# Query loads in 1 KB rows with the decay applied in the cast, plain copies of the retention's output, and another order of the first loads

## The chip, the cores and the metric

The kernel runs on one core of a Trainium2 chip. The metric is device time in microseconds (us) of one execution: the median of the runs is 292.84 us (three runs, 292.4 to 293.26). The engines are TensorE (PE in the profile, PEld for its weight loads), VectorE (DVE), ScalarE (ACT), GpSimd (POOL) and SyncE (SP), which issues most of the DMAs.

## The reference, cut to what matters

```
scores = (q @ k.T) / sqrt(64)                        # 8 batches, 8 heads, 576 tokens, head size 64
gamma  = 1 - 2 ** (-5 - h)                           # one decay for each head
D      = gamma ** (i - j) for i >= j, else 0
attn   = (scores * D) @ v
x      = attn, heads side by side: 4608 tokens x 512
out    = relu(x @ w_in) ** 2 @ w_out                 # 512 -> 2048 -> 512
```

The factor gamma ** (i - j) is a product of gamma ** i, which belongs to the query's token, and gamma ** -j, which belongs to the key's. The key's part is multiplied into v while v is cast to 16 bits (line 375, line 408). The query's part can be applied to the query before the matmuls or to the output after them, since it is one factor for each token and head. A retention over long rows is carried by a state per head (the sum of k.T v so far), which is decayed by gamma ** 128 from one block of 128 tokens to the next.

## The kernel before

**Tiling.** A unit is one batch's block of 128 tokens, or the last 64 tokens of two batches together ("tail"). There are 36 units, in 18 groups of two, numbered 0 to 17. Groups 0 to 3 are "paired" (lines 391 and 456): one load brings two units in rows of 512 B, and TensorE transposes k and q. From group 4 on each unit has its own loads of k, q and v (`add_load`, line 284; 256 KB each in rows of 256 B), GpSimd casts all three (`add_unit`, line 357), and one DMA transposes k and q together into `kqT` (line 388).

**The work of one group on TensorE.** The retention is four kinds of small matmuls on quarters of the array, all issued in `quad` (line 348): scores into `psc`, masked by VectorE into `rT` (line 676); state sums into `psS`, added and decayed by VectorE (lines 695 to 703 and 449); outputs of both the state and the masked scores into `psO`, which VectorE multiplies by gamma ** i and casts into `xT` (line 732; line 565 for the paired groups). Then the feed-forward: 64 matmuls `ph` of 256 columns with w_in (line 856), for each pair of banks a Relu and a Square on ScalarE (lines 864 and 874; one Square in eight is on VectorE, line 876), and the product with w_out. Group 0 makes that product plainly: 32 matmuls of 512 columns (line 896) and two ScalarE copies of its output (line 903). Groups from `STRASSEN = 1` on use Strassen's scheme (`add_strassen`, line 912): seven products of 8 matmuls with 256 columns (line 948), 56 in all, with sums `gS` of activations on VectorE (line 925), differences `wT` of w_out made once on VectorE (line 808), and copies and additions of partial results (lines 961, 971, 1022).

**What sets the order.** `Schedule` (line 15) is a planner in Python: every task has an engine, a duration, dependencies and resources (the eight PSUM banks are the resource `ff`), and the order that comes out is written into the program, one fixed order for each engine. An instruction can wait in its engine's queue but not be overtaken. So a late operand holds up all that stands behind it on that engine.

**The first loads.** `FIRST` is the order in which the planner issues the pair loads of groups 0 to 3 (k0, q0, v0 for group 0, k2 for group 1, k4 for group 2, k6 for group 3) on SP's queue and the eight weight pieces (w0 to w3 of w_in, w4 to w7 of w_out, 1 MB of 32-bit values each, cast to 16 bits on the way) on POOL's queue. `AFTER` makes a transfer wait for another's landing, so that they share the DMA engines in the wished order:

```
FIRST = ["k0", "q0", "v0", "k2", "q2", "v2", "w0", "w1", "w2", "k4", "q4", "v4", "w3", "w4", "w5", "w6", "w7", "k6", "q6", "v6"]
AFTER = {0: ("v", 0), 3: ("k", 4), ("k", 4): 0, ("k", 6): 5}
```

That is: w0 behind v0, w3 behind k4, k4 behind w0, k6 behind w5. At the start of the program TensorE fills its waits with 34 matmuls on zeros (line 251).

Of the kernel before, what the change touches and what calls it, by code (L numbers as in the profile page):

```python
# [103 lines left out]
def kernel(  # L104
# [9 lines left out]
    nc = tc.nc  # L114
# [24 lines left out]
    STRASSEN = 1  # L139
# [38 lines left out]
    vdec = {}  # L178

    def make_vdec(kind, pos):  # L180
        t = const.tile([P, H], FP32, name=f"vdl_{kind}")
        nc.vector.tensor_scalar(out=t, in0=lnrow, scalar1=pos, scalar2=None, op0=ALU.mult)
        d = const.tile([P, H], FP32, name=f"vdec_{kind}")
        nc.scalar.activation(out=d, in_=t, func=ACTF.Exp, bias=lnscale, scale=1.0)
        vdec[kind] = d
    make_vdec("full", iota_p)
# [9 lines left out]
    heads = [(4 * n + 2 * a + b, n, a, b) for n in range(2) for a in range(2) for b in range(2)]  # L196
    lncol = const.tile([P, NP], FP32, name="lncol")
    lnrow_R = const.tile([P, NP], FP32, name="lnrow_R")
    for h, n, a, b in heads:
        nc.vector.memset(lncol[64 * b:64 * b + 64, 2 * n + a:2 * n + a + 1], lng[h])  # L200
        nc.vector.memset(lnrow_R[64 * a:64 * a + 64, 2 * n + b:2 * n + b + 1], lng[h])

    mask = const.tile([P, 64], FP32, name="mask")
    nc.gpsimd.memset(mask, 1.0)
    for c in range(2):
        nc.gpsimd.affine_select(out=mask[c * 64:(c + 1) * 64], in_=mask[c * 64:(c + 1) * 64],
                                compare_op=ALU.is_ge, fill=0.0, base=0, pattern=[[1, 64]], channel_multiplier=-1)
# [9 lines left out]
    for hp in range(NP):  # L217
        nc.scalar.activation(out=gam_f[:, hp, :], in_=iota_f, func=ACTF.Exp, scale=lncol[:, hp:hp + 1])
    gam = {"full": gam_f.rearrange("p n (c i) -> p c n i", c=2),
           "tail": gam_f[:, :, 0:64].rearrange("p n (c i) -> p c n i", c=1).to_broadcast([P, 2, NP, 64])}  # L220
# [7 lines left out]
    SPREAD = 0.1  # L228
    SQ_LATE = (1, 4, 6)
# [4 lines left out]
    FIRST = ["k0", "q0", "v0", "k2", "q2", "v2", "w0", "w1", "w2", "k4", "q4", "v4", "w3", "w4", "w5", "w6", "w7", "k6", "q6", "v6"]  # L234
    AFTER = {0: ("v", 0), 3: ("k", 4), ("k", 4): 0, ("k", 6): 5}
# [36 lines left out]
    def dma_task(key, dur, fn, deps2=(), **kw):  # L272
        t = add("SP", key, dur, fn, deps=list(last_load) + list(deps2), **kw)
        last_load[:] = [t]
        return t
# [8 lines left out]
    def add_load(u):  # L284
        kind, b, c = units[u]
        for n, (name, src) in enumerate((("k", k), ("q", q), ("v", v))):
            def fn(name=name, src=src):
                x = ld.tile([P, H, D], FP32, name=f"{name}32", tag=f"{name}32")
                tile_of[name + "32", u] = x
                if kind == "full":  # L290
# [5 lines left out]
            loaded[name, u] = dma_task(0, 1.2 if loaded else 2.1, fn, acq=("ld",) if n == 0 else ())  # L296

    def add_load_pair(name, u):
        n = "kqv".index(name)

        def fn():
# [5 lines left out]
            if (name, u) in AFTER:  # L307
                behind(t, tile_of["w", AFTER[name, u]])
            tile_of["load", name, u] = t
        kw = dict(deps2=[wcast[AFTER[name, u]][0]]) if (name, u) in AFTER else {}  # L310
        loaded[name, u] = loaded[name, u + 1] = dma_task(0, 1.81 if loaded else 2.9, fn, acq=("wst",) if name != "q" else (),
                                                         after=2.1 + LAG.get(name + str(u), 0.0), **kw)
# [3 lines left out]
    def add_weight(i):  # L316
        fb = i % 4

        def fn():
# [3 lines left out]
            if i in AFTER:  # L323
                behind(tile_of["w", i], tile_of[("load",) + AFTER[i]])
        issue = add("POOL", -90 + i, 0.9, fn, deps=issues[-1:] + ([loaded[AFTER[i]]] if i in AFTER else []),
                    lag=0.0 if i in AFTER else 1.0)
# [30 lines left out]
    def add_unit(u, base):  # L357
# [4 lines left out]
        def sorted_cast(op, out_, in_):  # L362
            op(out=out_.rearrange("p (n b a d) -> p n b a d", n=2, b=2, a=2),  # L363
               in_=in_.rearrange("p (n a b) d -> p n b a d", n=2, a=2))
# [5 lines left out]
        def fq():  # L370
            sorted_cast(nc.gpsimd.tensor_copy, tile_of["kq", u][:, 1], tile_of["q32", u])
# [7 lines left out]
        cq = add("POOL", base + 1, 0.62, fq, deps=[loaded["q", u], ck])  # L379
# [11 lines left out]
    def add_unit_pair(u, base):  # L391
# [4 lines left out]
        for i, name in enumerate("kqv"):  # L396
            xs[name] = []
            for e in range(2):
# [3 lines left out]
                def fc(name=name, e=e, eng=eng):  # L402
# [8 lines left out]
                    else:  # L411
                        engines[eng](out=t.rearrange("p (n b a d) -> p n b a d", n=2, b=2, a=2),
                                     in_=x.rearrange("p (n a b) d -> p n b a d", n=2, a=2))
# [42 lines left out]
    def add_ret_pair(g):  # L456
# [29 lines left out]
        def fk():  # L486
            ps = rT["sum"] = banks("psS")
            for hp in range(NP):
                for e in range(2):
                    for s, a in ((0, 0), (1, 1), (0, 1), (1, 0)):  # L490
                        h = 4 * (hp // 2) + 2 * a + hp % 2
# [32 lines left out]
        def inter(other):  # L524
            for n in range(2):
                for a, b in ((0, 0), (1, 1), (0, 1), (1, 0)):
                    s = a ^ other
                    if s or carry:
                        x = 2 * n + b
                        put2(s, 4 * n + 2 * a + b, before(s)[half(a), half(x)], kqT(s)[half(a), NP + x, :], a)  # L530
# [7 lines left out]
        def fo1():  # L538

            tile_of["psO", g] = banks("psO")  # L540
            for m in range(NP):
                for e in range(2):
                    for s, b in ((0, 0), (1, 1), (0, 1), (1, 0)):
                        h = 2 * m + b
                        put2(s, h, tile_of["vx", u][half(s), e, 64 * h:64 * h + 64],
                             rT[e][half(s), m % 2, 2 * (m // 2) + b, :], s)
# [47 lines left out]

    def emit_scores(g):

        tile_of["psc", g] = banks("psc")
        for s, u in enumerate(units_of(g)):
            kT = tile_of["kqT", u]
# [488 lines left out]
```

## Time and profile before

| What | Before |
|---|---|
| Median of the runs | 292.84 us |
| The profiled execution's own time | 292.84 us |
| Its span, first to last instruction | 291.1 us |
| VectorE, ScalarE, GpSimd busy | 185.2, 188.4, 85.1 us |
| DMA packets, of them under 512 B | 139437, 118144 |
| Share of 16 DMA engines taken by SP's queue | 73.7% |
| TensorE's first matmul and last matmul's end | 1.3 and 286.9 us |
| Granted TensorE clock | 0.997 |

The span is what the profile accounts for; the 1.7 us beside it lie before the first and after the last instruction. The profile gives a matmul some 0.27 us, although the next one starts after 0.11 us, because matmuls overlap in the array. So a stall of TensorE is read from the distance between two starts, not from the sum of durations.

### The profile page before, as it was taken

How to read it: one execution, taken by the hardware profiler on the slowest of the kernel's cores; microseconds unless marked ns; L12 is line 12 of the kernel's file. 1: busy time of each engine (PE TensorE's matmuls, PEld its weight loads, DVE VectorE, ACT ScalarE, POOL GpSimd, SP SyncE). 2: the span in 40 equal slices, each digit the busy share in tenths (PEclk: the TensorE clock that was granted, in tenths of full speed). 3: DMA queues.
4: the chain of work that ended last, by engine and by line, in shares of the span. 5: the costliest groups of instructions: out<-in, count | busy, mean ns of one | idle time of the engine just before them, and what ended most of it. 6: DMA issues, size and time to landing. Idle time of an engine off the chain costs nothing.

```text
span 291.1 us, 10058 instructions
## 1 busy us (share of the span) xinstructions
PE 282.5 (97%) x4346; PEld 235.7 (81%) x4346; DVE 185.2 (64%) x392; ACT 188.4 (65%) x363; POOL 85.1 (29%) x121
## 2 busy tenths in 40 slices
PE   8999899999999999999999999999999999999994
PEld 3568647788878889888888888888888888888883
DVE  3773588778475748556768757576787675455632
ACT  5459769734867575867766667585767676747830
POOL 5615306352343433252515142525141400000000
PEclk9999999999999999999999999999999999999998
DMA  7999999999899889999969698999896720202004
GB/s 200 275 226 235 177 253 250 215 220 170 220 202 231 179 178 201 190 211 221 189 150 213 112 233 182 202 222 207 193 183 181 164 75 2 74 2 74 0 6 141
DMA packets 139437, 49.94 MB, mean 172 GB/s; under 512 B 118144, under 2 KB 135040, under 8 KB 139392
## 3 DMA queue, kind: packets, MB, share of 16 engines
q1 hardware_dynamic: 134848, 44.84, 73.7%
q0 software_dynamic: 4224, 4.19, 9.2%
q8 instruction: 34, 0.56, 0.8%
q10 hardware_dynamic: 320, 0.26, 0.4%
q14 instruction: 11, 0.09, 0.1%
HBM read 36.70 MB, written 9.44 MB: 158 GB/s over the span
## 4 chain that ended last, share of the span: by engine, by line
PE 70%; DVE 1%; issue 0%; DVEq 0%
PE ph L856 34%; PE po L948 31%; PE psO L349 3%; PE psS L349 1%; PE psc L349 1%; DVE o L971 0%; DVE rT L676 0%; DVE p L1000 0%; DVEq L971 0%
## 5 line engine op out<-in xcount | busy, mean ns | idle before, releaser
L856 PE MATMUL ph<-xT,w_in 128*128 128x256 f16 x1152 | 139.7, 273 | 0.8 <-DMA w_in<-in_moe_w_in_dram 0.8
L856 PEld LDWEIGHTS <-w_in 128*128 128x128 f16 x1152 | 110.5, 98 | 15.3 <-DMA w_in<-in_moe_w_in_dram 1.4
L864 ACT ACTIVATE rl<-ph 128x512 f16<-128x512 f32 x144 | 84.6, 588 | 51.2 <-PE ph L856 49.8
L874 ACT ACTIVATE gT<-rl 128x512 f16<-128x512 f16 x118 | 74.4, 630 | 3.4
L948 PEld LDWEIGHTS <-gS 128*128 128x128 f16 x544 | 52.5, 98 | 6.4
L948 PE MATMUL po<-wT,gS 128*128 128x256 f16 x408 | 54.9, 273 | 0.0
L925 DVE TENSOR_TENSOR gS<-gT 128x512 f16<-128x512 f16 x68 | 35.5, 524 | 15.6 <-ACT gT L874 15.6
L948 PEld LDWEIGHTS <-gT 128*128 128x128 f16 x408 | 39.3, 98 | 5.6 <-issue 0.8
L925 DVE TENSOR_TENSOR gS<-gT,gS 128x512 f16<-128x512 f16 x68 | 31.0, 459 | 12.5 <-ACT gT L874 10.6
L948 PE MATMUL po<-w_out,gT 128*128 128x256 f16 x272 | 36.7, 273 | 0.6 <-DVE rT L676 0.6
L363 POOL CAST kq<-k 128x512 f16<-128x512 f32 x28 | 19.3, 690 | 51.0 <-DMA k<-in_k_dram 49.7
L375 POOL TENSOR_TENSOR v<-v,vdec_full 128x512 f16<-128x512 f32 x24 | 25.4, 1058 | 29.5 <-DMA v<-in_v_dram 27.9
L961 ACT COPY u<-po 128x256 f32<-128x256 f32 x34 | 12.5, 369 | 23.9 <-PE po L948 23.7
L363 POOL CAST kq<-q 128x512 f16<-128x512 f32 x28 | 18.1, 647 | 30.6 <-DMA q<-in_q_dram 30.1
L971 DVE TENSOR_TENSOR o<-po,u 128x256 f32<-128x256 f32 x33 | 13.9, 421 | 15.9 <-PE po L948 9.6
L732 DVE TENSOR_TENSOR xT<-psO,gam_full 128x512 f16<-128x512 f32 x28 | 18.1, 685 | 7.7 <-PE psO L349 7.6
L676 DVE TENSOR_TENSOR rT<-psc,mask 128x512 f16<-128x512 f32 x28 | 18.3, 683 | 3.2 <-PE psc L349 3.0
L971 DVE TENSOR_TENSOR o<-po,p 128x256 f32<-128x256 f32 x18 | 7.6, 423 | 18.4 <-ACT u L961 11.9
L876 DVE TENSOR_TENSOR gT<-rl 128x512 f16<-128x512 f16 x26 | 12.7, 489 | 9.3 <-ACT rl L864 9.0
L948 PE MATMUL po<-w_out,gS 128*128 128x256 f16 x136 | 18.2, 273 | 0.0
L948 PE MATMUL po<-wT,gT 128*128 128x256 f16 x136 | 17.7, 273 | 0.0
L478 DVE TENSOR_TENSOR rx<-psc,mask 128x512 f16<-128x512 f32 x16 | 10.1, 683 | 3.7 <-PE psc L349 3.7
(78 smaller groups left out, 217.2 us busy)
## 6 DMA issues: line engine op xcount, KB each, us to landing
out_dram<-o SPq DMA_DIRECT2D x32, 256.0 KB, 3.1
k<-in_k_dram SPq DMA_DIRECT2D x24, 256.0 KB, 4.2
q<-in_q_dram SPq DMA_DIRECT2D x24, 256.0 KB, 4.9
v<-in_v_dram SPq DMA_DIRECT2D x24, 256.0 KB, 4.8
pair<-in_k_dram SPq DMA_DIRECT2D x4, 512.0 KB, 5.6
pair<-in_q_dram SPq DMA_DIRECT2D x4, 512.0 KB, 8.3
pair<-in_v_dram SPq DMA_DIRECT2D x4, 512.0 KB, 7.9
w_in<-in_moe_w_in_dram POOLq DMA_DIRECT2D x4, 512.0 KB, 8.4
```

Of the source, the lines that this page charges most:

```text
L349: t = nc.tensor.matmul(out_, lhsT=lhsT, rhs=rhs, start=start, stop=True, skip_group_check=True, tile_position=(64 * row, 64 * col))
L363: op(out=out_.rearrange("p (n b a d) -> p n b a d", n=2, b=2, a=2), in_=in_.rearrange("p (n a b) d -> p n b a d", n=2, a=2))
L375: nc.gpsimd.tensor_tensor(out=t, in0=tile_of["v32", u], in1=vdec[kind].rearrange("p (h o) -> p h o", o=1).to_broadcast([P, H, D]), op=ALU. ...
L676: tile_of["masking", g] = nc.vector.tensor_tensor(out=tile_of["rT", g][:, :, a], in0=tile_of["psc", g][a].rearrange("p (s n i) -> p s n i" ...
L732: nc.vector.tensor_tensor(out=tile_of["x", g].rearrange("p n (s c i) -> p c s n i", s=n, c=2)[:, c], in0=tile_of["psO", g][c].rearrange("p ...
L856: nc.tensor.matmul(tile_of["ph", g, fb][:, j, :], lhsT=w_in16[:, m, fi * P:(fi + 1) * P], rhs=tile_of["x", g][:, m, :], start=(m == 0), st ...
L864: nc.scalar.activation(out=t, in_=tile_of["ph", g, fb], func=ACTF.Relu)
L874: nc.scalar.activation(out=t, in_=rl, func=ACTF.Square)
L876: nc.vector.tensor_tensor(out=t, in0=rl, in1=rl, op=ALU.mult)
L925: nc.vector.tensor_tensor(out=Sx(k, h), in0=in0(h), in1=in1(h), op=op)
L948: nc.tensor.matmul(tile_of["pb", g, bank], lhsT=left(i), rhs=right[:, i, :], start=(start and i == 0), stop=(i == HF - 1), skip_group_chec ...
L971: nc.vector.tensor_tensor(out=o_tile(u)[:, half * HM:(half + 1) * HM], in0=bank(x), in1=tile_of[name, g], op=ALU.add)
```

## The change

Six things change together.

1. **q of the later units** (from group 4 on, tails excepted) is loaded by four DMAs in place of one. Each brings two heads (x and x + 4) to 32 partitions, four consecutive tokens to a partition, in rows of 1 KB.
2. **The cast of q** on GpSimd becomes a multiplication by gamma ** i (a table `qdec`), and sorts the four tokens apart. The cost of making the tables is a few small instructions at the start.
3. **The output of the retention** therefore needs no multiplication for these groups: `psO` leaves as two plain copies, the first on ScalarE (`X_ACT = (0,)`), the second on VectorE. For full units a copy reads `psO` in the order in which it lies and writes every fourth element, since the queries of a block now stand sorted by token modulo 4. For the same reason the queries that a small matmul reads (`qT`) are four runs of 16 elements, 256 B apart, in place of one run of 64, and the mask for full units has another pattern (and 16-bit ones).
4. **Which heads share a tile** changes from (4n + 2a + b) to (4a + 2n + b) in all index expressions; the paired groups' casts keep their shape.
5. **The first loads**: k4, q4, v4 go from between w2 and w3 to behind w7, and k4 waits for the landing of w5; the other waits but that of w0 are dropped.
6. **`STRASSEN`** goes from 1 to 2: group 1 too makes its product with w_out plainly.

```
-    STRASSEN = 1
+    STRASSEN = 2
...
+    X_ACT = (0,)
...
-    FIRST = ["k0", "q0", "v0", "k2", "q2", "v2", "w0", "w1", "w2", "k4", "q4", "v4", "w3", "w4", "w5", "w6", "w7", "k6", "q6", "v6"]
-    AFTER = {0: ("v", 0), 3: ("k", 4), ("k", 4): 0, ("k", 6): 5}
+    FIRST = ["k0", "q0", "v0", "k2", "q2", "v2", "w0", "w1", "w2", "w3", "w4", "w5", "w6", "w7", "k4", "q4", "v4", "k6", "q6", "v6"]
...
+                if kind == "full" and name == "q":
+                    for j in range(NP):
+                        nc.sync.dma_start(out=x[32 * j:32 * j + 32].rearrange("r (a t) d -> r a (t d)", a=2),
+                                          in_=src[b, :, c * P:(c + 1) * P, :].rearrange("(a x) (r t) d -> x r a (t d)", a=2, t=4)[j])
+                elif kind == "full":
                     nc.sync.dma_start(out=x, in_=src[b, :, c * P:(c + 1) * P, :].rearrange("h p d -> p h d"))
...
-            if (name, u) in AFTER:
-                behind(t, tile_of["w", AFTER[name, u]])
+            if (name, u) == ("k", 4):
+                behind(t, tile_of["w", 5])
...
         def fq():
-            sorted_cast(nc.gpsimd.tensor_copy, tile_of["kq", u][:, 1], tile_of["q32", u])
+            x, t = tile_of["q32", u], tile_of["kq", u][:, 1]
+            order = "p (x a d) -> p a x d" if kind == "tail" else "p (t a d) -> p a t d"
+            nc.gpsimd.tensor_tensor(
+                out=t.rearrange(order, a=2, d=D), in0=x.rearrange("p (a x) d -> p a x d", a=2),
+                in1=qdec[kind].rearrange("p (a x o) -> p a x o", a=2, o=1).to_broadcast([P, 2, NP, D]), op=ALU.mult)
...
+    def qT(u, a, x, c):
+        t = tile_of["kqT", u][half(a), NP:]
+        return t[:, x, half(c)] if units[u][0] == "tail" else t[:, :, 32 * x + 16 * c:32 * x + 16 * c + 16]
...
-                    quad(ps[a][half(c), hp, :], kT[half(a), hp, half(c)], kT[half(a), NP + hp, half(c)], a, c)
+                    quad(ps[a][half(c), hp, :], tile_of["kqT", u][half(a), hp, half(c)], qT(u, a, hp, c), a, c)
...
-                nc.vector.tensor_tensor(
-                    out=tile_of["x", g].rearrange("p n (s c i) -> p c s n i", s=n, c=2)[:, c],
-                    in0=tile_of["psO", g][c].rearrange("p (s n i) -> p s n i", s=n, i=64),
-                    in1=gam[units[us[0]][0]][:, c].rearrange("p (s n) i -> p s n i", s=1).to_broadcast([P, n, NP, 64]), op=ALU.mult)
-            x = add("DVE", key + 0.1 * c, 0.7, fx, deps=[t2] + ([x] if c else []), acq=() if c else ("x",))
+                x = tile_of["x", g].rearrange("p n (s c i) -> p c (n s) i", s=n, c=2)[:, c]
+                y = tile_of["psO", g][c].rearrange("p (n i) -> p n i", i=64)
+                if units[us[0]][0] == "full":
+                    x = x.rearrange("p n (r t) -> p n t r", t=4)
+                    y = y.rearrange("p n (t r) -> p n t r", t=4)
+                (nc.scalar.copy if c in X_ACT else nc.vector.tensor_copy)(out=x, in_=y)
+            x = add("ACT" if c in X_ACT else "DVE", key + 0.1 * c, 0.7, fx, deps=[t2] + ([x] if c else []), acq=() if c else ("x",))
```

## The prediction

> **What bounds the kernel now.** I read the busy times and the chain that ended last, then TensorE's own waits, then its timeline.
>
> ```profile
> PE 282.5 (97%) x4346; PEld 235.7 (81%) x4346; DVE 185.2 (64%) x392; ACT 188.4 (65%) x363; POOL 85.1 (29%) x121
> PE 70%; DVE 1%; issue 0%; DVEq 0%
> ```
>
> TensorE is busy for 97% of the span, and the chain runs through its matmuls. All other engines, and the DMAs, count only where they make TensorE wait. The list of its waits is short:
>
> ```profile
> PE warm L251 <- DVE wT L163: 1.3, 1, 1.3
> PE ph L856 <- DMA w_in<-in_moe_w_in_dram: 0.8, 1, 0.8
> PE po L948 <- DVE rT L676: 0.6, 1, 0.6
> PE psS L349 <- POOL vx L408: 0.5, 1, 0.5
> PE psT L427 <- DVE qx L412: 0.2, 1, 0.2
> ```
>
> Only the second and third fall after TensorE has begun real work (17.68 us); before that, matmuls on zeros fill its waits. Durations overlap, so I measure stalls between starts, in the timeline (start, length, count):
>
> ```profile
> 22.12 6.30 PE L856 MATMUL ph<-xT,w_in 128*128 128x256 f16 x56
> 30.49 0.61 PE L856 MATMUL ph<-xT,w_in 128*128 128x256 f16 x4
> 31.89 1.92 PE L856 MATMUL ph<-xT,w_in 128*128 128x256 f16 x16 [0.80 <-DMA w_in<-in_moe_w_in_dram]
> ...
> 34.98 1.03 PE L896 MATMUL po<-w_out,gT 128*128 128x512 f16 x4
> 39.41 5.47 PE L896 MATMUL po<-w_out,gT 128*128 128x512 f16 x23
> 46.46 0.61 PE L427 MATMUL psT<-ident,kx 128*128 128x128 f16 x8
> 47.78 0.86 PE L427 MATMUL psT<-ident,qx 128*128 128x128 f16 x8
> ...
> 80.91 0.60 PE L948 MATMUL po<-wT,gS 128*128 128x256 f16 x4
> 82.09 1.03 PE L948 MATMUL po<-w_out,gT 128*128 128x256 f16 x8 [0.59 <-DVE rT L676]
> ```
>
> One step of 256 columns is (6.30 - 0.27) / 55 = 0.1096 us, one of 512 columns (1.03 - 0.38) / 3 = 0.217. So the stalls are: w3 late, 31.89 - 30.49 - 4 x 0.11 = 0.96; inside the 23 matmuls with w_out, 5.47 - 22 x 0.217 - 0.38 = 0.32; q6's cast late, 0.86 - 0.61 = 0.25; a mask late, 82.09 - 80.91 - 0.44 = 0.74. Together **2.3 us**. Elsewhere the steps are regular to the end.
>
> **The parts, one by one.** The profiled execution took 292.84 us, which is also the median; its span is 291.1.
>
> *Plain product for group 1.* 32 steps of 0.217 = 6.94 in place of 56 of 0.1096 = 6.14: **+0.8 us** of TensorE, nothing beside which it could hide. The eight `gS` additions and seven copies and sums of partial results that go are VectorE's and ScalarE's, off the path.
>
> *The order of the first loads.* It takes away the cause of the first three stalls (1.5 us): w3 no longer waits for k4, and k6, q6 no longer come last behind w7 with VectorE on `wT`. The mask's stall may go too, as VectorE's work shifts. What is late next? TensorE's order in the changed program is the same up to 22.12 us, then: 28 `ph` steps, reaching w3 at 25.2; 24 more, w4 at 27.8; 4 plain and 20 `ph`, w5 at 30.9; 4 and 16, w6 at 33.5; 4, 12 and 2, w7 at 36.1; 18 plain, the transposes of k4 at 40.0. Landings in the trace: w0 17.16, w1 19.57, w2 22.52, and, with little beside them, w4, w5, w6 at 34.39, 37.10, 39.65, a step of 2.63. From w1 this gives w3 to w7 at 24.8, 27.5, 30.1, 32.7, 35.4; from w2, 0.3 later. Each is in time, w3 and w4 by 0.0 to 0.4. For k4 the trace has its image: k6 waited for w5 (37.10) with w6 and w7 in flight, and its transposes began at 46.46, 9.4 later, those of q6 ran on at 48.2, 11.1 later, the casts of v6 ended at 49.9, 12.8 later. Behind w5 at 30.1 to 30.4 these become 39.5 to 39.8 (reached at 40.0), 41.2 to 41.5 (41.6), 42.9 to 43.2 (42.9): at worst 0.3 late. With w's largest step, 3.08 (w7, pair traffic beside it), w7 would be 1.8 late. New stall here: 0 to 1.9, taken 0.3, as the closer rows say.
>
> *q in four DMAs.* TensorE meets this only through `kqT`. In group 4 the second transpose landed at 60.4 and the scores began at 64.04; from group 8 on the distance is about 10 us. In the changed order group 4's scores come at about 62.1, 1.9 sooner, and its loads too: w5 is 6.9 sooner, three more pairs at 1.65 (24.21, 26.0, 27.49) stand in front. So the margin stays 3.6, less two slower casts (0.8), less SP's issues. SP issues a plain load in 0.36 to 0.62 us when nothing holds it, so 6 more for a group are 2.2 to 3.7 us; but its issues there last up to 4 us because the rings are full, so most should hide. Worst 0.8 late, taken 0. Later, the SP queue's own waits between 100 and 240 us sum to 46 us; the 20 units issued there add at most 20 x 3 x 0.62 = 37, and the 10 us margin covers the rest.
>
> *The cast becomes a multiplication; copies for outputs.*
>
> ```profile
> L363 POOL CAST kq<-q 128x512 f16<-128x512 f32 x28 | 18.1, 647 | 30.6 <-DMA q<-in_q_dram 30.1
> L375 POOL TENSOR_TENSOR v<-v,vdec_full 128x512 f16<-128x512 f32 x24 | 25.4, 1058 | 29.5 <-DMA v<-in_v_dram 27.9
> L732 DVE TENSOR_TENSOR xT<-psO,gam_full 128x512 f16<-128x512 f32 x28 | 18.1, 685 | 7.7 <-PE psO L349 7.6
> L695 DVE CAST Rm<-psS 128x512 f16<-128x512 f32 x3 | 2.0, 679 | 0.0
> ```
>
> GpSimd gains 28 x 0.41 = 11.5 us, inside the 30 us that it waits for q. On VectorE a copy out of PSUM costs what the multiplication did (679 against 685 ns), so it saves only the 14 that move to ScalarE, 9.6 us; ScalarE takes 14 x 0.59 = 8.3 (a Relu out of PSUM takes 588 ns). No matmul follows `xT` closely: 0. The scattered write is not in the trace; even double, 0.6 us more for a copy, it hides in the 4 us of matmuls that follow `psO`. The mask costs the same.
>
> *Queries read in four runs of 16.* No matmul of the trace reads so. 384 scores and 400 - 64 = 336 products with states do it after the change, 720.
>
> ```profile
> L349 PE MATMUL psc<-kqT 64*64 64x64 f16 x448 | 6.2, 194 | 0.0
> L349 PE MATMUL psc<-kqT 64*64 64x128 f16 x128 | 3.3, 221 | 0.1
> ```
>
> Free at one end; at the other it costs what twice the columns cost, 25.8 - 13.8 = 12 ns each, **8.6 us**. I take 0, as the same 64 elements lie in whole runs. The Trainium skill (SBUF — State Buffer, Door 1, its note on cachelines) says that SBUF is read in lines of 16 bytes at full rate if each line is hit at least twice; runs of 32 bytes would then be free, and no run here shows that yet.
>
> **Sum.** 292.84 + 0.8 - 2.3 + new stalls. I take 0.6: 0.3 at the start and 0.3 for a late mask, between 0 and 0.74. That is **291.9 us**, 0.9 (0.32%) less. With no new stall it is 291.3, the floor.
>
> **The rivals.**
>
> - *The start runs late.* w3 to w7 land with the larger step, or SP's added issues delay group 4. New stalls of 1.2 to 1.9 + 0.8 + 0.74 = 3.4, so 292.5 to 294.8. For it: margins of 0.0 to 0.4 on w3 and w4. Against: the 2.63 step held for three landings.
> - *The queries' runs cost TensorE time* (the other side). From 2.5 ns for each of the 720 (0.9 + 0.9 = 1.8 us) on, the kernel is slower by over 0.3%; the end is 291.9 + 8.6 = 300.5. For it: nothing can hide it. Against: no element more is read.
> - *GpSimd's longer instruction holds up VectorE.* In the trace the additions of line 925 took 0.58 us on average when GpSimd was at work beside them, 0.38 otherwise, and the mask's stall of 0.74 came right after such ones. If the longer q multiplication makes this happen in each of the 14 later groups it costs up to 10.4 us; I put it at 2 to 5, so 293.3 to 296.3. Against: VectorE loses 9.6 us of work. The Trainium skill (SBUF — State Buffer, Who interferes with whom) has the rule behind it: a VectorE instruction with two SBUF inputs contends with a GpSimd one that reads SBUF; it speaks against the change.
> - *The loads gain nothing and SP becomes the bound* after group 8: 294 to 296, if 37 us do not fit into 46.
>
> **How the numbers follow.** Differences under 0.3% (0.9 us) are about what a measurement of this kernel can't tell from no change. Forecast case (291.3 to 292.5) 0.50, late start 0.20, costly runs 0.11, held-up VectorE 0.14, SP 0.05. Faster by over 0.3% (under 291.96) takes 0.37 of the first and 0.01 of others, 0.38; within, 0.13 of the first, 0.15 of the late start and 0.05 of the rest, 0.33; slower, 0.29. Range: the floor less 0.2 for rounding, 291.1, to 295.6, which leaves out most of the costly runs and the worst of VectorE and SP.
>
> **What would show it.** Right: TensorE's step from 22.12 us on unbroken, no wait on w_in, `po` line 896 64 times at 0.217; the small matmuls of scores at 13.8 ns each as before; `xT` copies of 0.68 and 0.59 us; transposes of q still some 10 us ahead. Wrong: TensorE waiting for w_in, `kqT` or `rT` more than once, or the rows of line 349 grown.

## The result, and the profile after

The changed kernel takes **296.03 us** (median of 4 runs, 294.91 to 296.62) against 292.68 for the kernel before beside it (4 runs): ratio 1.0107, 95% interval 1.0073 to 1.0142. It is **slower by 1.1%**, above the predicted range. The profiled execution is the fastest of the four, 294.91 us with a span of 292.9, so what follows accounts for 2.1 us of the 3.35.

Busy times and the chain that ended last, from the page of the changed kernel:

```profile
PE 282.9 (97%) x4322; PEld 234.1 (80%) x4322; DVE 186.0 (64%) x375; ACT 203.4 (69%) x378; POOL 99.0 (34%) x128
PE 67%; DVE 5%; ACT 4%; issue 0%; DVEq 0%
```

The chain leaves TensorE more often than before: 5% of it is now VectorE's and 4% ScalarE's. The list of TensorE's waits (us in total, times, longest) says where:

```profile
PE po L982 <- DVE rT L708: 1.4, 1, 1.4
...
PE ph L890 <- DVE rT L708: 0.8, 1, 0.8
PE psS L373 <- DVE vx L436: 0.6, 1, 0.6
PE po L982 <- DVE gS L959: 0.5, 2, 0.3
...
```

No wait for w_in, w_out or the cast of q6 is left. All waits shown are for VectorE. Two are left out: that for the zeros of the first matmuls (1.3 us) is as before, and one of 0.2 us is for a cast of k (`kx`). TensorE's timeline of the changed kernel (start, length, count) gives their sizes between starts, and shows the start running as forecast:

```profile
21.60 5.85 PE L890 MATMUL ph<-xT,w_in 128*128 128x256 f16 x52
...
35.12 4.48 PE L930 MATMUL po<-w_out,gT 128*128 128x512 f16 x20
...
47.76 0.20 PE L373 MATMUL psS<-vx,kx 64*64 64x64 f16 x2
48.55 0.41 PE L373 MATMUL psS<-vx,kx 64*64 64x64 f16 x28 [0.59 <-DVE vx L436]
...
64.62 0.60 PE L982 MATMUL po<-wT,gS 128*128 128x256 f16 x4
66.58 1.03 PE L982 MATMUL po<-w_out,gT 128*128 128x256 f16 x8 [1.36 <-DVE rT L708]
...
125.15 0.60 PE L890 MATMUL ph<-xT,w_in 128*128 128x256 f16 x4
125.90 0.61 PE L982 MATMUL po<-wT,gS 128*128 128x256 f16 x4 [0.15 <-DVE gS L959]
...
170.71 1.04 PE L982 MATMUL po<-w_out,gT 128*128 128x256 f16 x8
172.56 0.60 PE L890 MATMUL ph<-xT,w_in 128*128 128x256 f16 x4 [0.81 <-DVE rT L708]
```

In the first part every step is 0.11 or 0.217 us and nothing is late: 52 `ph` run past w3 without a break, and 20 products with w_out from 35.12 us on run without one too. The stalls are: `vx` late, 0.78; masks late at 65 us, 66.58 - 64.62 - 0.44 = 1.52; `gS` late at 125 us, 0.31, and likewise 0.23 and 0.48 at 140 and 155; masks late at 171 us, 172.56 - 170.71 - 0.88 = 0.97. Together **4.3 us**, where the prediction took 0.6. With them its own sum is 292.84 + 0.8 - 2.3 + 4.3 = 295.6. The execution in which these stalls were read took 294.91, 0.7 less: TensorE's first real matmul came 0.3 us sooner (17.36 for 17.68 us), and gaps of under 0.2 us between its starts, which the sum does not count, add up to about 0.9 us less than before.

The groups that the change touched, from the list of groups of the changed kernel (busy us, mean ns of one, idle before):

```profile
L397 POOL TENSOR_TENSOR kq<-q,qdec_full 128x512 f16<-128x512 f32 x24 | 27.1, 1131 | 50.3 <-DMA q<-in_q_dram 50.2
L769 DVE CAST xT<-psO 128x512 f16<-128x512 f32 x14 | 16.8, 1203 | 1.3 <-PE psO L373 1.3
L769 ACT CAST xT<-psO 128x512 f16<-128x512 f32 x14 | 16.7, 1194 | 9.6 <-PE psO L373 9.6
L373 PE MATMUL psc<-kqT 64*64 64x64 f16 x448 | 6.2, 194 | 0.0
```

Two things stand out. The copies cost twice what was expected (1.2 us for 0.68 and 0.59), so VectorE's 14 take 16.8 us where 9.6 were expected. Its sum is 186.0 us where it was 185.2, and not 9.6 us less: 7.2 us came back in these copies and 6.9 in longer additions (the table below), while group 1 needs fewer instructions. And the small matmuls with the queries in four runs cost exactly what they did, 194 ns by the record.

A look into VectorE's timeline of the changed kernel, just ahead of the late `gS`:

```profile
122.61 0.42 DVE L959 TENSOR_TENSOR gS<-gT 128x512 f16<-128x512 f16 x1
122.95 1.26 DVE L959 TENSOR_TENSOR gS<-gT,gS 128x512 f16<-128x512 f16 x1
...
124.58 1.26 DVE L959 TENSOR_TENSOR gS<-gT,gS 128x512 f16<-128x512 f16 x1
```

and GpSimd's of the same moments (`kq` is q's multiplication, `v` that of v):

```profile
122.65 1.28 POOL L397 TENSOR_TENSOR kq<-q,qdec_full 128x512 f16<-128x512 f32 x1 [4.95 <-DMA q<-in_q_dram]
124.52 1.04 POOL L403 TENSOR_TENSOR v<-v,vdec_full 128x512 f16<-128x512 f32 x1 [0.59 <-PE ph L890]
```

An addition that takes 0.42 us alone takes 1.26 when it meets a multiplication on GpSimd, and ends 0.28 us after it: 124.21 after 123.93, 125.84 after 125.56. The new multiplication of q and the old one of v come one behind the other, and catch two additions running. The kernel before has this beside v alone, as here just ahead of the mask's stall of 0.74 us (an addition on VectorE, and v on GpSimd):

```profile
78.30 1.26 DVE L925 TENSOR_TENSOR gS<-gT,gS 128x512 f16<-128x512 f16 x1
78.11 1.17 POOL L375 TENSOR_TENSOR v<-v,vdec_full 128x512 f16<-128x512 f32 x1
```

**Theory 1**: the doubled copies make VectorE late. **Theory 2**: GpSimd's longer instruction on q holds up VectorE's additions (a rival of the prediction). **Theory 3**: the loss lies in the start. Their numbers stand with the runs.

### The profile page after: what moved, and what is told of

The parts are those of the page before. It is cut to its first block, busy times and chain, and to the rows that moved or that the text cites. A ratio compares the mean times of both kernels' runs of the same rounds, so it can differ in the third digit from the quotient of the medians.

```text
span 292.9 us, 10131 instructions
## 1 busy us (share of the span) xinstructions
PE 282.9 (97%) x4322; PEld 234.1 (80%) x4322; DVE 186.0 (64%) x375; ACT 203.4 (69%) x378; POOL 99.0 (34%) x128
## 4 chain that ended last, share of the span: by engine, by line
PE 67%; DVE 5%; ACT 4%; issue 0%; DVEq 0%
PE po L982 31%; PE ph L890 30%; PE psO L373 3%; DVE gS L959 3%; ACT gT L908 2%; ACT rl L898 2%; PE psS L373 1%; PE psc L373 1%; ACT xT L769 1%; DVE gT L910 1%; DVE rT L708 0%; DVE o L1005 0%; DVE p L1034 0%; DVEq L1005 0%
## 5 line engine op out<-in xcount | busy, mean ns | idle before, releaser
L982 PEld LDWEIGHTS <-gS 128*128 128x128 f16 x512 | 49.4, 98 | 7.2 <-DVE gS L959 1.4
L982 PE MATMUL po<-wT,gS 128*128 128x256 f16 x384 | 52.6, 273 | 0.5 <-DVE gS L959 0.5
L959 DVE TENSOR_TENSOR gS<-gT,gS 128x512 f16<-128x512 f16 x64 | 34.2, 535 | 26.0 <-ACT gT L908 25.4
L397 POOL TENSOR_TENSOR kq<-q,qdec_full 128x512 f16<-128x512 f32 x24 | 27.1, 1131 | 50.3 <-DMA q<-in_q_dram 50.2
L982 PEld LDWEIGHTS <-gT 128*128 128x128 f16 x384 | 37.2, 98 | 6.0 <-issue 1.5
L982 PE MATMUL po<-w_out,gT 128*128 128x256 f16 x256 | 34.5, 273 | 1.4 <-DVE rT L708 1.4
L387 POOL CAST kq<-k 128x512 f16<-128x512 f32 x28 | 18.8, 671 | 28.4 <-DMA k<-in_k_dram 27.6
L769 ACT CAST xT<-psO 128x512 f16<-128x512 f32 x14 | 16.7, 1194 | 9.6 <-PE psO L373 9.6
L910 DVE TENSOR_TENSOR gT<-rl 128x512 f16<-128x512 f16 x26 | 14.1, 543 | 12.5 <-ACT rl L898 12.4
L769 DVE CAST xT<-psO 128x512 f16<-128x512 f32 x14 | 16.8, 1203 | 1.3 <-PE psO L373 1.3
L708 DVE TENSOR_TENSOR rT<-psc,mask_full 128x512 f16<-128x512 f32 x24 | 16.1, 681 | 0.4 <-PE psc L373 0.3
L930 PE MATMUL po<-w_out,gT 128*128 128x512 f16 x64 | 15.8, 380 | 0.0
```

The source lines that it names most:

```text
L397: nc.gpsimd.tensor_tensor(out=t.rearrange(order, a=2, d=D), in0=x.rearrange("p (a x) d -> p a x d", a=2), in1=qdec[kind].rearrange("p (a x ...
L708: tile_of["masking", g] = nc.vector.tensor_tensor(out=tile_of["rT", g][:, :, a], in0=tile_of["psc", g][a].rearrange("p (s n i) -> p s n i" ...
L769: (nc.scalar.copy if c in X_ACT else nc.vector.tensor_copy)(out=x, in_=y)
L910: nc.vector.tensor_tensor(out=t, in0=rl, in1=rl, op=ALU.mult)
L930: nc.tensor.matmul(tile_of["po", u], lhsT=tile_of["g", g][:, fi, s * P:(s + 1) * P], rhs=w_out16[:, fi, :], start=(fi == 0), stop=(fi == N ...
L959: nc.vector.tensor_tensor(out=Sx(k, h), in0=in0(h), in1=in1(h), op=op)
```

## The experiments

All ratios are to the kernel before on the same chip, in brackets the 95% interval. "Lost in additions" is what all `gS` and `gT` instructions on VectorE took beyond 0.42 us each, summed over the profiled execution. Stalls are read between TensorE's starts and counted from 18 us on, from 0.2 us each; regular gaps between the two groups of products into `psO` are left out.

| Kernel | Median us | Ratio | Lost in additions, us | Stalls for VectorE, us |
|---|---|---|---|---|
| before | 292.68 | 1 | 11.5 | 0.75 (and 1.5 for loads and a cast) |
| changed | 296.03 | 1.0107 [1.0073, 1.0142] | 18.4 | 4.3 |
| e1_read | 295.23 | 1.0077 [1.0052, 1.0102] | 18.8 | 4.2 |
| e2_flat | 294.98 | 1.0070 [1.0044, 1.0096] | 19.6 | 3.8 |
| e4_cast | 293.30 | 1.0003 [0.9986, 1.0020] | 14.1 | 1.3 |
| e5_bstart | 291.81 | 0.9959 [0.9942, 0.9975] | 12.6 | 1.2 |
| e8_ones | 293.73 | 1.0013 [0.9997, 1.0029] | 22.3 | 2.8 |
| e9_cast_read | 292.95 | 0.9981 [0.9968, 0.9995] | 12.5 | 2.2 |
| e10_gam | 292.12 | 0.9961 [0.9945, 0.9977] | 12.4 | 2.0 |
| e11_qhalf | 294.58 | 1.0042 [1.0021, 1.0064] | 18.8 | 4.1 |
| e12_vhalf | 291.57 | 0.9935 [0.9916, 0.9953] | 10.3 | 0.8 |
| e13_gam_vhalf | 291.52 | 0.9933 [0.9915, 0.9951] | 9.7 | 1.8 |
| e14_all | 292.78 | 0.9979 [0.9962, 0.9995] | 15.0 | 2.0 |
| e15_read_dve | 295.15 | 1.0073 [1.0046, 1.0099] | 16.7 | 4.3 |
| e16_gam_ones | 294.42 | 1.0053 [1.0033, 1.0073] | 16.8 | 3.0 |
| e17_ones_dur | 294.40 | 1.0033 [1.0011, 1.0056] | 22.9 | 2.2 |
| e18_cast_read_dve | 292.38 | 0.9978 [0.9957, 0.9998] | 11.3 | 2.7 |
| e3_start | 293.24 | 1.0005 [0.9983, 1.0027] | 19.7 | 1.5 |
| e20_loads | 295.31 | 1.0076 [1.0049, 1.0104] | 21.4 | 4.6 |
| e19_plain | 298.82 | 1.0182 [1.0138, 1.0226] | 15.9 | 6.0 |

The stalls are of one profiled execution each, which may be 1 us off the median of its kernel (those of e4_cast and e3_start are the fastest of their kernels); the ratios decide.

Four kernels leave something out and compute another result: e2_flat the reordering of the tokens, e4_cast, e9_cast_read and e18_cast_read_dve the decay of the query. In e1_read, e2_flat, e4_cast, e9_cast_read and e11_qhalf the planner's durations are those of the changed kernel, and with them the order of the tasks.

### The copies: e1_read and e2_flat

```
-                    x = x.rearrange("p n (r t) -> p n t r", t=4)
-                    y = y.rearrange("p n (t r) -> p n t r", t=4)
+                    x = x.rearrange("p n (r t) -> p n r t", t=4)     # e1_read; e2_flat has neither line
+                    y = y.rearrange("p n (t r) -> p n r t", t=4)
```

> The changed kernel, but the xT copies of the full units walk their output in its own order (runs of 4 r + t, unbroken 2-byte writes) and take the step of 16 floats on the PSUM side instead. Nothing is left out. Theory 1 (the 8-byte step of the 2-byte writes doubled the copies, 1.19 and 1.20 us in the mean where 0.59 and 0.68 were expected, and the 0.6 us more in each group on VectorE and on ScalarE make masks and state additions late): the copies fall to 0.6 on ScalarE and 0.7 on VectorE, the stalls of TensorE from 120 us on (0.5 before gS, 0.97 before the masks at 171 us, some more) go, the one at 65 us stays since no copy has run by then; 296.0 - 2.0 = about 294.0 us. Theory 2 (GpSimd's q multiplication, 1131 ns for 647, holds up VectorE): the copies may get shorter but the stalls stay, 295.5 to 296.0. Theory 3 (the cost is in the start): 295.5 to 296.0. If it is the reordering itself and not the side that carries the step, the copies stay at 1.2 and the time at 296.0.

> The changed kernel, but the xT copies do not reorder at all (unbroken on both sides); the reordering of the tokens is left out, so that the rows of the output stand in another order. Theory 1: as with the step on the PSUM side, about 294.0 us, copies 0.6 and 0.7; if a step on the PSUM side costs too, only this kernel has the short copies. Theories 2 and 3: 295.5 to 296.0 although the copies are short.

The copies of the kernel with unbroken writes, from its list of groups:

```profile
L769 DVE CAST xT<-psO 128x512 f16<-128x512 f32 x14 | 9.6, 682 | 1.3 <-PE psO L373 1.3
L769 ACT CAST xT<-psO 128x512 f16<-128x512 f32 x14 | 8.2, 582 | 9.5 <-PE psO L373 9.5
```

The step on the write side was what doubled them; a step of 16 floats on the PSUM side costs nothing (682 and 582 ns; unbroken on both sides 683 and 583). But 15.7 us of shorter copies bring only 0.3% and 0.4%, less than the intervals can tell, and the stalls stay (4.2 and 3.8 us). Theory 1 as the main cause falls.

### GpSimd's multiplication: e4_cast, then e9_cast_read

```
-            nc.gpsimd.tensor_tensor(out=t.rearrange(order, ...), in0=x.rearrange(...), in1=qdec[kind]..., op=ALU.mult)
+            nc.gpsimd.tensor_copy(out=t.rearrange(order, a=2, d=D), in_=x.rearrange("p (a x) d -> p a x d", a=2))
```

> The changed kernel, but GpSimd casts q of the units from 6 on by a plain copy; the decay of the query is left out there. Theory 2 (the longer multiplication with two inputs in SBUF holds up VectorE's additions): the cast is about 0.65 us, GpSimd's sum falls by about 12 us, gS additions go from 543 to about 460-524 ns in the mean, the stall at 65 us (1.5) and half of the others go; 296.0 - 2.5 = about 293.5 us. Theory 1: the copies stay at 1.2 us, the stalls at 120-172 us stay, that at 65 us may go; 294.5 to 296.0. Theory 3: 296.0.

> The changed kernel with both: GpSimd's plain cast of q (the decay of the query is left out in the units from 6 on) and the xT copies with the step on the PSUM side (0.58 and 0.68 us). What is left of the change is the start, the loads of q in rows of 1 KB, the query's order and the copy on ScalarE. If theory 2 carries nearly all of the loss and the copies a little (295.23 against 296.03), 296.0 - 2.7 - 0.8 = 292.5 us; if nothing else costs, the 291.8 us of the start alone; 293.3 or more would mean that the copies' length costs nothing and something of the loads or the order costs 1.5 us.

The plain cast alone takes the ratio from 1.0107 to 1.0003: **1.04%, 3.0 us**, the whole loss against before. The longest of TensorE's waits in the kernel with the plain cast (that for the zeros left out):

```profile
PE psT L453 <- DVE kx L438: 0.9, 1, 0.9
PE po L980 <- DVE rT L706: 0.5, 1, 0.5
...
PE ph L888 <- DVE rT L706: 0.2, 1, 0.2
...
```

The waits for masks fall from 2.2 to 0.7 us in sum, and those for `gS` are gone from the list. That for `kx` lies at 6.4 us, as its 0.2 us did in the changed kernel, ahead of the first real matmul (17.47 us for 17.36), so it does not count. The copies in it still take 1.2 us. Theory 2 holds. With short copies as well it is 0.9981, another 0.2%, which the intervals can't tell. That the decay is left out is not the reason: e10_gam (below) casts q plainly too, leaves nothing out and stands at 0.9961.

### The same multiplication elsewhere, and in pieces: e8_ones, e11_qhalf

```
# e8_ones, in the kernel with the changed start alone
-            sorted_cast(nc.gpsimd.tensor_copy, tile_of["kq", u][:, 1], tile_of["q32", u])
+            nc.gpsimd.tensor_tensor(out=..., in0=tile_of["q32", u]..., in1=ones..., op=ALU.mult)
# e11_qhalf, in the changed kernel
+            for a in range(2):
+                nc.gpsimd.tensor_tensor(out=t.rearrange(order, ...)[:, a], in0=x...[:, a], in1=qdec[kind][:, 4 * a:4 * a + 4]..., op=ALU.mult)
```

> The kernel with the changed start alone (291.8 us, 0.996 of the kernel before), and in it GpSimd's cast of q from unit 6 on is a multiplication with a tensor of ones: the same numbers, nothing left out, only the longer instruction with two inputs (28 times about 1.1 for 0.67 us). Theory 2 (that instruction holds up VectorE's additions of two fp16 tiles) puts the loss here without the loads, the copies and the query order of the change: as much as the plain cast gave back in the changed kernel, 291.8 + 2.7 = 294.5 us (293.5 to 295), gS and gT additions beside it at 0.75 us and up to 1.3, the stalls before gS and the masks as in the changed kernel. If the loss needs the copies, too, so that VectorE has no slack left (theory 1), it stays at 291.5 to 292.3.

> The changed kernel with GpSimd's multiplication of q in two instructions of four heads, about 0.55 us each, so that the same work is done in pieces. Theory 2a (VectorE's addition waits until the GpSimd instruction that holds the port has ended): beside q the additions last at most about 0.42 + 0.55 = 1.0 us, where they last up to 1.27, and 0.65 in the mean for 0.79; the time falls by 0.5 to 1.5 us, to about 295. Theory 2b (both share the bandwidth, whatever the length): the same mean, 296.0 us, or a little more by the second instruction's fixed cost. Theory 1: 296.0.

Put into the kernel with the new start alone, the multiplication by ones costs 1.0013 - 0.9959 = 0.54%, 1.6 us: about half of the loss appears without the copies and the new loads of q, less than the 2.7 us that were expected. In halves, in the changed kernel, the same work gives 0.65% back, 1.0107 to 1.0042, and these intervals do not touch. VectorE's timeline of the kernel with halves, at the same place as above:

```profile
123.67 0.83 DVE L960 TENSOR_TENSOR gS<-gT,gS 128x512 f16<-128x512 f16 x1
...
125.29 1.15 DVE L960 TENSOR_TENSOR gS<-gT,gS 128x512 f16<-128x512 f16 x1
```

The addition beside the first half of q (0.69 us on GpSimd in the mean) takes 0.83 us, the one beside the undivided v still 1.15. Over the run the longest addition beside q falls from 1.265 to 0.857 us. So VectorE waits for the end of an instruction, and does not share a rate with it (theory 2a). The sum lost in additions did not fall (18.8): more of them meet a piece, each for less time.

### The start: e5_bstart, e3_start, e20_loads, e19_plain

```
# e5_bstart: the kernel before, with these; e3_start: the changed kernel, without them
-    STRASSEN = 1
+    STRASSEN = 2
-    FIRST = [... "w2", "k4", "q4", "v4", "w3", ... "w7", "k6", "q6", "v6"]
-    AFTER = {0: ("v", 0), 3: ("k", 4), ("k", 4): 0, ("k", 6): 5}
+    FIRST = [... "w2", "w3", ... "w7", "k4", "q4", "v4", "k6", "q6", "v6"]     # w0 behind v0, k4 behind w5
# e20_loads: the changed kernel with the old FIRST and AFTER only; e19_plain: with STRASSEN = 1 only
```

> The kernel before with the start of the changed one alone: the plain product for groups 0 and 1, the weights w0 to w7 in one row ahead of k4, q4 and v4, and without the waits between loads that this order does not need. Theory 3 (the start costs): + 0.8 for the plain product of group 1, + 0.8 for a late vx, and little of the 2.3 us of stalls won back: 294 to 295 us. Theories 1 and 2 (the start is worth about nothing or a small gain): 292.7 + 0.8 + 0.8 - 0.96 - 0.32 - 0.25 = about 292.7, at most 293.3 us, with the late w_in (0.96), the late w_out (0.32) gone from the rows of TensorE.

> The changed kernel with the start of the kernel before (both products of groups 1 and on in the seven-product form, k4, q4 and v4 between w2 and w3); nothing left out. By the start alone in the kernel before (0.9959) the start is a gain of 0.41%, and this one stands at 1.0107 + 0.0041 = 1.015 of before; with the waits for w3 and w_out back in TensorE's rows. If the start hides stalls only where VectorE has slack, it stays at 1.011.

> The changed kernel with the plain product for group 1 and the old order of the first loads (k4, q4, v4 between w2 and w3, with their waits); nothing left out. If the order of loads is what brings the loss out: 1.0005 + 0.8/293 = 1.003 of before, up to 1.006 if w_in for group 1 comes late; if the plain product is: 1.010 or more.

> The changed kernel with the seven-product form for group 1 again, and with the new order of the first loads; nothing left out. If the plain product is what brings the loss out (0.8 us of matmuls more, less work for VectorE in group 1, so that every later group stands otherwise to the loads): 1.001 of before. If the order of loads is: 1.0107 - 0.8/293 = 1.008.

| | old start | new start |
|---|---|---|
| the rest as before | 1 | 0.9959 |
| the rest changed | 1.0005 | 1.0107 |

The new start alone is a gain of 0.41%, where e5_bstart was expected at none. But in the changed kernel it is a loss of 1.0%, against what I expected of e3_start (1.015). **The loss is one of the two together.** With the old start the rest of the change, the longer multiplication in it, costs nothing that the interval (up to 1.0027) can tell, and the new start alone is a gain. What the multiplication costs apart with the old start is not shown: no run has the plain cast there.

Of the start, either half alone brings out a loss in the changed kernel. The plain product of group 1 with the old loads takes 1.0005 to 1.0076, between what e20_loads was expected to show for either half; the new order of loads without the plain product takes it to 1.0182, above both numbers expected of e19_plain. That kernel has some 4.6 us of stalls between 40 and 49 us, most of them for `vx`, `kqT`, `rx` and `xT` of the paired groups. Its profiled execution (300.46 us) also shows a lower granted TensorE clock right after them, 0.88 from 40 to 50 us and 0.78 from 50 to 60, where the other profiles show 1.00: 22 matmuls of 256 columns from 48.7 us on start 0.21 us apart in place of 0.11, which makes 2.4 us of its loss. So its number does not give the price of the loads' order alone.

TensorE's waits in the changed kernel with the old start, the two longest behind that for the zeros:

```profile
PE po L985 <- DVE rT L711: 0.9, 1, 0.9
PE po L985 <- DVE gS L962: 0.3, 1, 0.3
...
```

Its additions lose as much as those of the changed kernel, 19.7 against 18.4 us, and it stalls for VectorE for 1.5 us and not 4.3. So the sum does not decide. Which additions are hit differs, at least at the place shown above (121 to 126 us there; VectorE's third addition in a row, and GpSimd's multiplication of q):

```profile
122.02 0.42 DVE L962 TENSOR_TENSOR gS<-gT,gS 128x512 f16<-128x512 f16 x1
122.10 1.24 POOL L400 TENSOR_TENSOR kq<-q,qdec_full 128x512 f16<-128x512 f32 x1 [5.40 <-DMA q<-in_q_dram]
```

The multiplication of q runs from 122.10 to 123.34, VectorE's three additions in a row are through at 122.44, and beside it only a `gT` instruction behind them is held up, by 0.23 us.

### What is left: e10_gam, e15_read_dve, e18_cast_read_dve, e16_gam_ones, e17_ones_dur

```
# e10_gam: changed kernel with the plain cast, and the decay back in the output's multiplication on VectorE
+                nc.vector.tensor_tensor(out=x, in0=y, in1=m, op=ALU.mult)      # y read as (t r), x written as (r t), m from gam_f
# e15_read_dve: e1_read with X_ACT = (); e18_cast_read_dve: e9_cast_read with X_ACT = ()
# e16_gam_ones: e10_gam with the multiplication of q by ones on GpSimd
# e17_ones_dur: e8_ones with 1.06 for 0.62 as the planner's duration of it
```

> The changed kernel with the decay of the query put back into the xT multiplication on VectorE, which reads psO in the order of tokens (step of 16 floats) and writes unbroken; GpSimd casts q plainly. Start, loads of q in rows of 1 KB and query order stay; nothing is left out. By theory 2 it stands near the start alone: 291.8, with up to 0.7 us more if the strided reading makes the multiplication longer than 0.685; lower than 291.8 (to 291.3) if the loads in 1 KB rows are worth something. By theory 1 alone (length of the copies) it gains the same; a time of 293 or more would say that the loads or the order cost.

> The changed kernel with the unbroken writes of the xT copies and both copies on VectorE; nothing left out. ScalarE loses 14 copies of 0.58 us, VectorE gets 14 of 0.68. If the 0.6 us by which the kernel with short copies and the plain cast is above the start alone is ScalarE's, the time falls from 1.0077 to about 1.005 of before, and gT stands less behind on ScalarE; if ScalarE's share is harmless and VectorE is the engine that is late, it rises to 1.010.

> The changed kernel with plain cast of q (its decay left out in the units from 6 on), unbroken xT writes and both xT copies on VectorE. Against the same with one copy on ScalarE (0.9981): 0.996 if ScalarE's 8 us are what is left above the kernel with the decay on VectorE (0.9961); 0.998 if not.

> The kernel with changed start, 1 KB rows of q and the decay in the xT multiplication on VectorE (0.9961 of before), where GpSimd multiplies q by a tensor of ones in place of the cast; nothing left out. If the rows and the query order make the multiplication dearer, it costs what it did in the changed kernel with short copies, 1.0077 - 0.9981 = 0.96%: 1.0057. If not, what it did in the start alone, 0.54%: 1.0015.

> The start alone with the multiplication by ones (1.0013 of before), and the cost that the planner knows for it set from 0.62 to 1.06 us, as the change has it; this moves instructions, nothing is left out. If the planned cost makes the difference between 0.54% and 0.96%, the time rises to 1.0055; if the plan is harmless 1.001; below 1.000 if a plan that knows the length goes round it.

With the decay on VectorE and everything else changed the ratio is 0.9961, that of the start alone (0.9959): the loads in 1 KB rows, the query order and the other pairing of heads together neither cost nor gain anything that the intervals can tell. Moving the copy from ScalarE to VectorE changes nothing in either pair (1.0077 and 1.0073; 0.9981 and 0.9978), so ScalarE's 8 us are not what leaves e9_cast_read 0.2% above e10_gam; that 0.2% is within the intervals and stays open.

The price of the multiplication differs with its surroundings: 0.54% in the start alone, 0.92% with the rows of 1 KB (1.0053 - 0.9961), 0.96% and 1.04% in the changed kernel. The intervals of e8_ones and e16_gam_ones do not touch; the kernel with the planner's duration (0.74%) lies between what was expected of it either way and can't be told from either. The additions lost 22.3 us in the first and 16.8 us in the dearer second: again the moment counts, and not the sum.

### Versions that beat both: e12_vhalf, e13_gam_vhalf, e14_all

```
# GpSimd's multiplication of v in two instructions of four heads each; e12 in e5_bstart, e13 in e10_gam
+            for a in range(2):
+                nc.gpsimd.tensor_tensor(out=t[:, 4 * a:4 * a + 4], in0=tile_of["v32", u][:, 4 * a:4 * a + 4], in1=vdec[kind][:, 4 * a:4 * a + 4]..., op=ALU.mult)
# e14_all: the changed kernel with q and v in halves, unbroken writes, X_ACT = ()
```

> The kernel with the changed start alone (0.996 of the kernel before), and GpSimd's multiplication of v in two instructions of four heads (24 + 4 units, 1.04 us each otherwise); nothing left out. Theory 2a (an addition on VectorE waits for the end of the GpSimd instruction): the longest additions fall from 1.26 to about 0.86 us as beside q in halves, and 0.3 to 1.0 us of the time goes: 0.993 to 0.995 of before. If what is left of the stalls there does not come from GpSimd, 0.996; if the second instruction's fixed cost (0.61 + 0.61 for 1.04) costs more, 0.996 to 0.998.

> The kernel with the changed start and the 1 KB rows of q, its decay in the xT multiplication on VectorE (0.996 of before), and GpSimd's multiplication of v in halves; nothing left out. As with the start alone: 0.993 to 0.995 by theory 2a, 0.996 otherwise. Against the start alone with halves it says again what the rows of 1 KB are worth (nothing, by the pair without halves).

> The change as it is meant, with what was found put right: decay of q on GpSimd in halves, v in halves, xT copies with unbroken writes, both on VectorE. Nothing left out. Theory 2a: 1.0107 - 0.003 (copies) - 0.0065 (q in halves) - 0.002 (v in halves) - 0.002 (ScalarE without copies) = about 0.997 of before; if ScalarE's share or the halves of v are worth nothing, 1.001. Below 0.995 would say that the decay on GpSimd can pay after all.

Halves of v gave 0.24% and 0.28%, the same twice, but each less than its two intervals can tell apart. The two best, 291.57 and 291.52 us, are 0.65% faster than before; neither has the decay of q on GpSimd. The change with everything put right reaches 0.9979, faster than before but not than its own start alone.

## Why the prediction was wrong, point by point

- **What bounds the kernel**: right. TensorE is busy for 97%, and only its stalls moved the time.
- **Start** (+0.8, -2.3 with the mask's 0.74, +0.3): right in sum when it stands alone, in part by luck. Predicted -1.2 us (292.84 to 291.6); the start alone gave 0.9959, 1.2 us less. The stalls for loads and for the cast of q6 went, and w3 to w7 were in time: in e5_bstart they landed at 24.95 to 35.54 us, where 24.8 to 35.4 was computed, and in the changed kernel some 1.6 us sooner. But the mask's stall did not go. In e5_bstart it is 1.20 us, at 66 us; gaps of under 0.2 us between TensorE's starts, which the prediction did not count, made up for it, about 1.2 us less in sum. The late `vx` of the changed kernel (0.78) was not foreseen.
- **q in four DMAs, SP**: right, 0. TensorE never waited for a late transpose of the later units.
- **Queries in four runs**: right, 0; the rows of line 373 are those of line 349 before.
- **Copies for outputs**: the duration was wrong, the verdict nearly right. They doubled, as the bound had it, and most of that did hide: shortening them gave 0.2 to 0.4% in three pairs, none of which is told from 0 alone. But "so it saves only the 14 that move to ScalarE, 9.6 us" fell, and with it the argument that I put against the third rival.
- **The step that failed** is "GpSimd gains 28 x 0.41 = 11.5 us, inside the 30 us that it waits for q". GpSimd had the time, as the 50 us of idle before line 397 show; the cost lies with VectorE, whose additions wait for the end of each such instruction and then make TensorE wait. The sum put this at 0, but for 0.3 us for a late mask; measured, with the new start, this step is worth 1.04%, 3.0 us. It was written down as a rival, at 2 to 5 us and 293.3 to 296.3, which holds the time, but with a chance of only 0.14. The trace had the evidence. Read one by one, the additions of line 925 that overlap a GpSimd instruction take 0.62 us in the mean and the others 0.42 (the prediction has 0.58 and 0.38). The mean hid it; single ones of 1.26 us beside v's multiplication were there, as shown above, and the change doubled the number of such instructions.
- **What is late next**: 0.6 us of new stalls was taken, 4.3 came. The sum treated start and cast as separate edits. The 2x2 table shows that they are not: 1.0005 - 1 and 0.9959 - 1 add up to 0.9964, and 1.0107 was measured.

How the new start brings the loss out is only partly settled. Shown, at one place, is that it shifts what meets what. Whether the shift comes from the moments at which loads land, or from the planner's other order of instructions, was not told apart.

## What to carry to other kernels

When work is added to GpSimd, ask not whether GpSimd has time but which VectorE instructions run beside it, and how long the longest single instruction is: two-input additions in SBUF waited here for its end. Splitting it into shorter ones gave 0.65% back, and with the decay in a VectorE instruction that reads PSUM anyway the loss was gone (0.9961). And parts of a change that shift work in time must be measured together; here one half alone was free within its interval, the other a gain, and both together cost 1.1%.

## What the runs showed of the hardware that I had not expected

- **Two-input additions on VectorE (both in SBUF) and GpSimd instructions exclude each other.** 0.42 us alone, up to 0.88 us beside casts (0.61), up to 1.3 beside a multiplication (1.04), up to 0.89 beside one in halves; the one that waits ends 0.28 us after the GpSimd instruction. It seems to go both ways: the multiplication at 122.65 took 1.28 us, 0.24 more than the shortest, as if it had had to wait for the addition at 122.61 that ran when it started. VectorE instructions with one input in PSUM are untouched: masks take 0.67 to 0.69 us, beside GpSimd or not. The Trainium skill (SBUF — State Buffer, Who interferes with whom) says this: whoever issues first gets the shared ports for the whole instruction and the other blocks. The runs agree, with these numbers.
- **16-bit writes with a step of 8 bytes halve the rate** of a copy out of PSUM, on VectorE (1.29 for 0.68 us) and ScalarE (1.30 for 0.58) alike, while a read of PSUM with a step of 64 bytes is free on both, and so is TensorE's read of queries in runs of 32 bytes. The Trainium skill (SBUF — State Buffer, Door 1, its note on cachelines) gives full rate from two hits in a line of 16 bytes; for these writes, with two in each line, the measurement differs and decides. For the runs of 32 bytes it agrees.
- **The sum lost to contention says little about the time**: the kernels that lose 19.7 and 22.3 us (e3_start, e8_ones) stand at 1.0005 and 1.0013, the one that loses 18.4 (changed) at 1.0107.
- **Long stalls of TensorE may cost more than their length**: behind 4.6 us of them in e19_plain the granted clock was 0.88 and then 0.78, and 22 matmuls started at half their rate, 2.4 us more. No other profile of this case shows it, and that the stalls were the cause is not shown.
